# Another order of the first head pair's units, with two of its PSUM copies on ScalarE

## The chip, the core and the metric

The kernel runs on one core of a Trainium2 chip. The metric is the device time of one execution in microseconds (us); lower is better. TensorE multiplies matrices, VectorE and ScalarE read its results out of PSUM, GpSimd does small work, and DMA engines move and transpose data. A "slot" below is one place in the program's order, filled by one short unit of TensorE work.

## The reference, cut to what matters

```python
xn = layernorm(x)                                   # 2048 x 640
q  = xn @ wq                                        # 32 heads of 192
p  = softmax(q @ k[last 512].T * 192 ** -0.5)
s  = (p @ v[last 512]) @ wo                         # summed over the heads
g  = silu((silu(xn @ w_gate) * (xn @ w_up)) @ w_down)
return x + s * g
```

The kernel does the FFN g first, then attention in 16 pairs of heads, adding each pair's product with wo to s. The sums for s lie in SBUF as f32: s_m (columns 0 to 511, three of four row blocks), s_t (the last 128 columns, transposed) and s_o (the last block).

## The kernel before

After the FFN, each pair has two parts: scores and exponentials for four blocks of 512 rows, then a stretch of small units of TensorE work in a fixed order. A unit's name has the block, the kind and the half. Kinds a and b are the product of the probabilities with V, for row tiles 0-1 and 2-3. Kinds w, x and y are output products with wo of the block two before: row tiles 0-1, row tiles 2-3, and the last 128 columns. 0e is a query product of the next pair, moved forward. In the first pair only blocks 0 and 1 have output products, so they carry the names 2w, 2x, 2y and 3w, 3x, 3y.

The two halves of a unit use the two halves of TensorE's rows and swap PSUM banks between them. GpSimd's tiny memset passes the word from one half to the next, so another unit has to stand between the halves.

```python
def part(p):                                        # in pv(i, q2): kinds a and b
    ...
    st["acc"] = sc_tile() if i < 2 and q2 else mm_tile()   # two buffers in each pool
    ...
    if p == 3:
        divide(i, q2, acc, (0, 1) if i < 2 and q2 else ())

def divide(i, q2, acc, by_dve):                     # softmax's division, then a DMA transpose
    ...
    nc.vector.reciprocal(r[:], a_v[:, :, :, Dh : Dh + 1])
    ... # four ScalarE activations, or two VectorE multiplications, into O_b
    nc.sync.dma_start_transpose(out=OT_b[:, 6 * q2 : 6 * q2 + 6, :], in_=O_b[...])

def add_sum(pr, to, ps):
    if pr == 0:
        nc.vector.tensor_copy(out=to, in_=ps)       # first pair: a copy
    else:
        nc.vector.tensor_tensor(to, to, ps, ALU.add)

def sum_rows(i, qts, sc):                           # at the end of w and x
    ...
    add_sum(pr, to, sc)

FIRST = """0a0 0b0 0a1 0b1 0e0 1b0 1a0 1b1 2b0 1a1 2b1 2w0 2x0 2w1 2a0 2x1 2a1 2y0 3a0 3y0 3a1 3x0
    3b0 3x1 3w0 3b1 3w1"""                          # LATER is the order of the other pairs
```

The softmax here doesn't subtract the row's maximum and nothing guards it: scores larger than these inputs give would overflow.

## Time and profile before

| quantity | before |
|---|---|
| median time (3 runs, then 6 with those beside the changed kernel) | 923.19 us, then 923.16 us |
| span of the profiled run | 921.8 us |
| TensorE / VectorE / ScalarE busy | 914.7 / 594.6 / 473.7 us |
| the stretch of the first pair, first V product to next query product | 190.74 to 210.40 us |

The page's first part gives busy times, its fourth the chain of work that ended last. In a timeline, a line gives start, length, engine, line of the program and how many instructions are merged; the bracket gives the idle time ahead of it and what ended that. TensorE's ends are modelled: two units that follow each other without a pause start 0.65 to 0.67 us apart and are each shown as 0.81 to 0.83 us long. So a bracket on TensorE understates a loss by about 0.17 us. The length of the whole stretch does not have this fault.

Two more lines of the kernel before matter. The first is the group of VectorE's copies into s_m (line, engine, work, count, then busy us and mean ns of one, then idle time before them). The second tells how long the eight transposes of the stretch took from issue to landing.

```profile
L630 DVE COPY s_m<-sc 128x1024 f32<-128x1024 f32 x6 | 7.3, 1224 | 5.7 <-PE sc L619 5.6
DMA to landing us min/median/max: 2.7/2.8/4.6
```

The change takes two of those six copies. One of the eight transposes took 4.6 us where the median is 2.8.

### The profile page before, as it was taken

What the parts mean: (1) busy time and instruction counts of PE and PEld (TensorE: products, weight loads), DVE (VectorE), ACT (ScalarE), POOL (GpSimd) and SP (SyncE); (2) the same over time, 40 slices, a digit from 0 to 9 for tenths busy, and PEclk for the clock granted to TensorE, in tenths of its full rate; (3) what the DMA queues carried; (4) which work ended last, traced back from release to release, by engine and by line L of the source; (5) the groups of instructions that cost most, each with busy time, mean ns of one, the idle gap of its engine ahead of it and who ended that gap; (6) DMA issues with size and microseconds to landing.
All of it is one profiled execution on the core that took longest, in us unless ns stands there. A gap on an engine that the chain in (4) does not pass through costs nothing.

```text
span 921.8 us, 23762 instructions
## 1 busy us (share of the span) xinstructions
PE 914.7 (99%) x10193; PEld 527.3 (57%) x10193; DVE 594.6 (65%) x844; ACT 473.7 (51%) x841; POOL 91.0 (10%) x302
## 2 busy tenths in 40 slices
PE   9999999999999999999999999999999999999998
PEld 5444445564747464656565656565656565555664
DVE  6443321467676777777777767676767676767656
ACT  4222222546464656565655565655556565556561
POOL 0000000000000000000000000000000000002977
PEclk9999999999999999999999999999999999999999
DMA  9312430045443425343534453435353434333535
GB/s 310 68 34 65 90 78 1 1 67 121 51 112 47 111 56 104 58 103 58 108 58 108 57 109 57 97 58 97 69 95 65 92 75 76 89 70 108 127 48 163
DMA packets 246969, 77.45 MB, mean 84 GB/s; under 512 B 227792, under 2 KB 246864, under 8 KB 246864
## 3 DMA queue, kind: packets, MB, share of 16 engines
q1 hardware_dynamic: 245376, 74.23, 39.3%
q8 instruction: 80, 1.31, 0.6%
q10 hardware_dynamic: 1488, 1.70, 0.6%
q14 instruction: 25, 0.20, 0.1%
HBM read 39.06 MB, written 2.62 MB: 45 GB/s over the span
## 4 chain that ended last, share of the span: by engine, by line
PE 98%; DMA 1%; DVE 0%; SPq 0%; POOLq 0%; POOL 0%; issue 0%; DVEq 0%
PE mm L460 22%; PE sc L474 18%; PE sc L619 16%; PE mm L499 16%; PE sc L282 11%; PE mm L321 6%; PE sc L587 3%; PE sc L579 2%; PE mm L551 2%; PE mm L579 1%; DMA x_t<-in_A_x_dram 1%; DMA OT_b<-O_b 1%; PE gu L282 0%; PE mm L330 0%; PE sc L551 0%; PE sc L499 0%
## 5 line engine op out<-in xcount | busy, mean ns | idle before, releaser
L478 ACT ACTIVATE p_t<-sc 128x1024 bf16<-128x1024 f32 x254 | 253.3, 1024 | 120.2 <-PE sc L474 120.2
L465 DVE TENSOR_REDUCE qT<-mm 128x512 bf16<-128x1024 f32 x189 | 231.2, 1223 | 98.9 <-PE mm L460 96.4
L529 ACT ACTIVATE O_b<-mm,r 128x192 bf16<-128x192 f32 x490 | 166.5, 423 | 190.4 <-issue 138.9
L460 PE MATMUL mm<-xnT,wq_p 64*128 64x512 bf16 x1890 | 234.9, 376 | 0.0
L474 PE MATMUL sc<-qT,khat 64*128 64x512 bf16 x1524 | 195.4, 376 | 0.0
L619 PE MATMUL sc<-wo_p,OT_b 64*128 64x512 bf16 (+1 forms) x1608 | 179.2, 345 | 1.2 <-DMA OT_b<-O_b 1.2
L499 PE MATMUL mm<-V_p,p_t 64*128 64x193 bf16 x3520 | 178.3, 242 | 0.0
L499 PEld LDWEIGHTS <-p_t 64*128 64x128 bf16 x3584 | 155.0, 93 | 34.6
L460 PEld LDWEIGHTS <-wq_p 64*128 64x128 bf16 x1890 | 91.8, 94 | 112.0 <-issue 0.7
L632 DVE TENSOR_TENSOR s_m<-s_m,sc 128x1024 f32<-128x1024 f32 x82 | 100.2, 1222 | 49.3 <-PE sc L619 43.0
L474 PEld LDWEIGHTS <-khat 64*128 64x128 bf16 x1536 | 74.8, 94 | 91.0
L619 PEld LDWEIGHTS <-OT_b 64*128 64x128 bf16 x1608 | 75.6, 94 | 46.2 <-DMA OT_b<-O_b 1.7
L605 POOL MEMSET turn_t<- 128x1 f32 x246 | 24.4, 99 | 699.1 <-PE mm L499 494.2
L290 DVE TENSOR_TENSOR hT<-sc,sg 128x512 bf16<-128x512 f32 x46 | 31.7, 692 | 81.6 <-ACT sg L289 81.6
L632 DVE TENSOR_TENSOR s_t<-s_t,sc 128x512 f32<-128x512 f32 x82 | 56.2, 686 | 18.3 <-PE sc L587 16.8
L289 ACT ACTIVATE sg<-sc 128x512 bf16<-128x512 f32 x46 | 27.4, 597 | 69.7 <-PE sc L282 68.2
L282 PE MATMUL sc<-xnT,wg_sb 128*128 128x512 bf16 (+1 forms) x260 | 60.2, 354 | 0.1
L282 PE MATMUL sc<-xnT,wu_sb 128*128 128x512 bf16 (+1 forms) x260 | 60.2, 354 | 0.0
L632 DVE TENSOR_TENSOR s_o<-s_o,sc 128x640 f32<-128x640 f32 x52 | 42.7, 821 | 15.9 <-PE sc L619 14.8
L321 PE MATMUL mm<-wd_sb,hT 128*128 128x512 bf16 (+1 forms) x240 | 46.7, 347 | 0.0
L518 DVE RECIPROCAL r<-mm 128x4 f32<-128x4 f32 x124 | 22.6, 182 | 33.1 <-PE mm L499 24.7
L282 PEld LDWEIGHTS <-wu_sb 128*128 128x128 bf16 x285 | 27.0, 98 | 27.1 <-issue 0.3
(94 smaller groups left out, 458.9 us busy)
## 6 DMA issues: line engine op xcount, KB each, us to landing
wo_p<-in_A_wo_dram SPq DMA_DIRECT2D x16, 480.0 KB, 4.9
K_p<-in_A_k_cache_dram SPq DMA_DIRECT2D x32, 192.0 KB, 4.6
V_p<-in_A_v_cache_dram SPq DMA_DIRECT2D x32, 192.0 KB, 3.1
wq_p<-in_A_wq_dram SPq DMA_DIRECT2D x64, 80.0 KB, 2.9
wq_p<-in_A_wq_dram SPq DMA_DIRECT2D x16, 160.0 KB, 3.2
x_t<-in_A_x_dram SPq DMA_DIRECT2D x14, 160.0 KB, 3.1
OT_b<-O_b SPq DMA_TRANSPOSE x124, 2.7
wd_sb<-in_B_w_down_dram SPq DMA_DIRECT2D x1, 1920.0 KB, 11.8
```

Of the source, the lines that this page charges most:

```text
L282: nc.tensor.matmul(out, w_sb[:, c, f * P : (f + 1) * P], xnT[:, c, qc], start=(c == 0), stop=(c == NC - 1),)
L290: nc.vector.tensor_tensor(hTs[b][:, f, :], u, sg[:], ALU.mult)
L321: nc.tensor.matmul(dn, at, by, start=(f == 0), stop=(f == NF - 1))
L460: nc.tensor.matmul(q_ps[:, h, :], pairs[pr]["wq"][r, c, j * P : (j + 1) * P], xnT[r, c, b * 512 : (b + 1) * 512], start=(c == 0), stop=(c ...
L465: nc.vector.reduce_sum(qTs[i][:, j, :], q_ps[:, :, :].rearrange("p h n -> p n h"), axis=AX.X)
L474: nc.tensor.matmul(sc[:, h, :], khat[r, j, ks], qT[r, j, :], start=(j == 0), stop=(j == 2))
L478: nc.scalar.activation(p_t[:, :, :], sc[:, :, :], ACT.Exp, scale=scale)
L499: m = nc.tensor.matmul(acc[:, k, h * 256 : h * 256 + Dh + 1], Ps[i][kc][r, h, qt * P : (qt + 1) * P], V_p[r, kc, h, 0 : Dh + 1], start=(p ...
L529: nc.scalar.activation(O_b[:, qt, h, :], a_k[:, h, 0:Dh], ACT.Copy, scale=r[:, k, h, :])
L579: nc.tensor.matmul(ps, OTs[i][:, 3 * qt + j, :], pairs[i // NB]["wo"][:, j, cols], start=(first and j == 0), stop=(end and j == 2),)
L619: m = nc.tensor.matmul(ps[:, k, 0 : cols.stop - cols.start], OTs[i][r, 3 * qt + j, :], pairs[i // NB]["wo"][r, j, cols], start=(turn == 0 ...
L632: nc.vector.tensor_tensor(to, to, ps, ALU.add)
```

## The change

The order of the first pair's units is changed so that the first row tiles of block 2 come ahead of its second ones, while block 3 starts with its second row tiles. The copies of 2x and 3x go to ScalarE, which has more idle time in this stretch. The diff, whole:

```diff
@@ sum_rows
-        add_sum(pr, to, sc)
+        if i < 2 and qts.start:
+            nc.scalar.copy(to, sc)
+        else:
+            add_sum(pr, to, sc)
@@
-    FIRST = """0a0 0b0 0a1 0b1 0e0 1b0 1a0 1b1 2b0 1a1 2b1 2w0 2x0 2w1 2a0 2x1 2a1 2y0 3a0 3y0 3a1 3x0
-        3b0 3x1 3w0 3b1 3w1"""
+    FIRST = """0a0 0b0 0a1 0b1 0e0 1b0 1a0 1b1 2a0 1a1 2a1 2w0 2x0 2w1 2b0 2x1 3b0 2b1 3x0 2y0 3x1 3b1
+        3a0 3y0 3w0 3a1 3w1"""
```

## The prediction

> **What bounds the kernel now.** I read the page from the top: busy shares, the chain that ended last, then the chain and the timelines of the one stretch that the change touches. The first line below is the busy share of the engines, the second is the start of the chain's shares by line.
>
> ```profile
> PE 914.7 (99%) x10193; PEld 527.3 (57%) x10193; DVE 594.6 (65%) x844; ACT 473.7 (51%) x841; POOL 91.0 (10%) x302
> ...
> PE 98%; DMA 1%; DVE 0%; SPq 0%; POOLq 0%; POOL 0%; issue 0%; DVEq 0%
> ```
>
> TensorE is busy for 914.7 of the 921.8 us of the span, and 98% of the chain that ended last is TensorE. VectorE, at 65%, and ScalarE, at 51%, do not bound it. A change that leaves TensorE's work as it is can win at most the 7.1 us in which TensorE idles, and most of that is the start and the end of the program. The change touches the value and output products of the first head pair only. This stretch runs once, between about 190.7 us (the first product with V_p) and 210.4 us (the next product with wq_p). The chain of waits there:
>
> ```profile
> 193.57 1.08 PE mm L460 x10
> 194.65 0.67 PE sc L499 x16
> 195.32 0.57 PE mm L499 x13
> 195.89 4.62 DMA OT_b<-O_b
> 200.51 0.05 issue
> 200.55 1.47 PE sc L619 x12
> ```
>
> One link is not TensorE's: the transpose of a block's divided outputs, issued at 195.89 us and landed 4.62 us later. The timeline of TensorE (start, length, work, and in brackets the idle time before it) shows what it costs and that nothing else is lost:
>
> ```profile
> 198.49 0.81 PE L619 MATMUL sc<-wo_p,OT_b 64*128 64x512 bf16 x6
> 200.55 1.47 PE L619 MATMUL sc<-wo_p,OT_b 64*128 64x512 bf16 x12 [1.25 <-DMA OT_b<-O_b]
> 201.86 0.83 PE L499 MATMUL mm<-V_p,p_t 64*128 64x193 bf16 x16
> 202.53 0.81 PE L619 MATMUL sc<-wo_p,OT_b 64*128 64x512 bf16 x6
> 203.17 0.83 PE L499 MATMUL mm<-V_p,p_t 64*128 64x193 bf16 x16
> ...
> 209.75 0.81 PE L619 MATMUL sc<-wo_p,OT_b 64*128 64x512 bf16 x6
> 210.40 1.24 PE L460 MATMUL mm<-xnT,wq_p 64*128 64x512 bf16 x10
> ```
>
> The idle time is 1.25 us, ahead of what the code calls 2x0, the first half of the output product of block 0's second two row tiles. Starts of neighbouring units are 0.65 us apart where the first is six output matmuls and 0.67 us where it is sixteen value matmuls. From 200.55 to 210.40 us lie nine of the one and six of the other: 9 x 0.648 + 6 x 0.667 = 9.83 us, against 9.85 us measured. So after the DMA wait there is no idle time left to remove. VectorE's and ScalarE's timelines of the same stretch:
>
> ```profile
> 202.06 2.54 DVE L630 COPY s_m<-sc 128x1024 f32<-128x1024 f32 x2 [3.18 <-PE sc L619]
> ...
> 208.64 1.22 DVE L630 COPY s_m<-sc 128x1024 f32<-128x1024 f32 x1 [1.10 <-PE sc L619]
> ...
> 210.60 1.22 DVE L630 COPY s_m<-sc 128x1024 f32<-128x1024 f32 x1 [0.47 <-PE sc L619]
> 211.74 1.21 DVE L465 TENSOR_REDUCE qT<-mm 128x512 bf16<-128x1024 f32 x1
> 204.73 1.36 ACT L529 ACTIVATE O_b<-mm,r 128x192 bf16<-128x192 f32 x4 [2.76 <-DVE r L518]
> ```
>
> The four VectorE copies are those that the change's condition picks from; ScalarE idles for 2.76 us in between, so it has room for two of them.
>
> **What the Trainium skill says.** "Perfetto Trace Analysis" (Identifying the Most-Contended Engine) says to optimize the engine with the most occupancy first, and that matmul busy time overstates how near the limit TensorE is. Here busy time is used only to find gaps, for which back-to-back starts suffice. "ScalarE: Activation LUTs" (What ACT_TABLE_LOAD costs) gives 0.833 ns per element and a fixed 186 ns when scale and bias are immediates, and its section Table sets: the hidden batching unit has copy in every set, so no table load is added. The trace of before agrees roughly: the exponentials of 128x1024 take 1025 ns at the median, casts of 128x512 from PSUM take 587 ns. "PSUM — Partial Sum Buffer" (Specifications (TRN2)) says ScalarE and VectorE can read PSUM in parallel if their banks do not collide; ScalarE's divisions and VectorE's copies overlap in this trace at unchanged lengths (the second copy of the pair at 202.06 us is 1.22 us as well). "Runtime: NRT & Kernel Launch" (Instruction fetch mechanics) says engines fetch instructions in blocks of 16 KiB, 256 instructions, through DMA. The packet records agree: the queue marked instruction moved 80 packets of 16 KB, and one of them, at 197.88 us, took 0.92 us in the middle of the late transpose. Eighteen of that transpose's 256-byte packets took 1.7 to 1.9 us, while the mean of packets in an undisturbed transpose is about 20 ns.
>
> **The change part by part.** A unit is written as block, kind, half: a and b are the value products of row tiles 0-1 and 2-3; w and x are output products of row tiles 0-1 and 2-3, y that of the last 128 columns, all three of the block two before the one in their name.
>
> Removed: two VectorE copies of 128x1024, 2 x 1.22 = 2.45 us of VectorE, those of 2x and 3x. Added: two ScalarE copies. From the cast and the exponential (1025 - 587) / 512 = 0.86 ns per element, so an estimate of 1.02 us each, 2.04 us of ScalarE. TensorE's instructions are the same in number and kind. Moved: 2a now runs where 2b ran and 2b where 2a ran or one place later; 3b and 3x come forward, 3a and 3y go back. Up to 2x1 each place holds a unit of the same length as before.
>
> The wait of 1.25 us: its transpose, the transposes ahead of it and the lengths of all units ahead of it are unchanged. The instruction orders compared, with their waits, give TensorE's first difference at row 2645, 68 rows after 2x0's first. The instruction fetch that delays the transpose follows TensorE's position in its own program, so it should fall at the same place. Gain: 0.
>
> After it, I lay the new order out from 200.55 us with the same unit times: 2x0 200.55, 2w1 201.21, 2b0 201.86, 2x1 202.53, 3b0 203.17, 2b1 203.84, 3x0 204.51, 2y0 205.16, 3x1 205.80, 3b1 206.45, 3a0 207.12, 3y0 207.78, 3w0 208.43, 3a1 209.08, 3w1 209.75, next pair 210.40. Each unit that opens a PSUM tile needs the tile two openings earlier in its pool read out. A unit's results are ready 0.81 us (outputs) or 0.83 us (values) after its start, and the reader starts 0.02 us later:
> - 2b0 (201.86) needs 1a divided: done 199.61, unchanged. 3b0 (203.17) needs 2a divided: ScalarE's four divisions start at 200.61, when the transpose lands, end 201.97. Slack 1.2 us.
> - 3x0 (204.51) needs 2w copied by VectorE: 202.06 + 1.22 = 203.29. Slack 1.2 us.
> - 2y0 (205.16) needs 2x copied by ScalarE: 202.53 + 0.83 + 1.02 = 204.38. Slack 0.8 us.
> - 3a0 (207.12) needs 2b divided: values ready 204.67, reciprocal to 204.87, four divisions of 1.36 us to 206.26. Slack 0.9 us.
> - 3y0 (207.78) needs 3x copied by ScalarE: 3x1 starts 205.80, the copy 206.63, and it ends 207.65. Slack 0.1 us. This is the tightest, and the only one tighter than before, where the shortest slack was that of 3x0 on 2y's copy and addition (206.47 - 206.13 = 0.3 us).
> - 3w0 (208.43) needs 2y copied and added: 205.99 + 0.69 + 0.69 plus 0.04 = 207.41. Slack 1.0 us.
> - The next pair's first product (210.40) needs 3b divided, 209.02, and the second (212.77) 3a divided, 211.6. Its second score tile (212.12) needs 3w copied by VectorE, 211.82, as now.
>
> Every one holds, so the stretch ends at 210.40 us again, and 3w's copy is still what VectorE does ahead of the next reduction at 211.74 us. Nothing after it has changed order. The 2.45 us taken from VectorE lie beside TensorE, as do the 2.04 us on ScalarE. Sum on the path: 0 us, with up to 0.15 us of wait ahead of 3y0 if the ScalarE copy takes 1.2 us like VectorE's. 923.19 + 0.0 = 923.2 us.
>
> **The rivals.**
> (1) A new wait takes the place of none: ScalarE's copy of 3x is late for 3y0. For it: the slack of 0.1 us is an estimate on a copy that no line of this trace has (f32 to f32). Against it: the exponential of the same shape is 1025 ns. It would make 923.3 to 923.5 us.
> (2) The 1.25 us wait goes or grows. The collision of the fetch with the transpose is a matter of tenths of a microsecond: the transpose's packets start at 197.08 and its undisturbed run is about 1.1 us, so a fetch 0.4 us later would miss it. Its usual time to landing is 2.8 us, which gives 198.7 instead of 200.51 us, before 2x0 could start at 199.14. That would make 923.19 - 1.25 = 921.9 us. For it: the runs of before lie 0.9 us apart (923.14 and 924.0), so something moves by that much. Against it: nothing ahead of that point changes, so both kernels should share it.
> (3) VectorE was holding PSUM tiles in this stretch and its relief shortens it by several tenths. For it: two copies back to back, 2.54 us. Against it: no idle time on TensorE between 200.55 and 210.40 us. It would make 922.9 us if it were so.
>
> **Range and chances.** The step that could matter is bounded by one stretch of 20 us in 923. The whole of it idle-free is worth -1.25 us, a new wait +0.15 us, and the spread of the runs of before is 0.9 us, upward. I put the range at 922.3 to 924.1 us. To leave the 2% band the time would have to move by 18.5 us, about the length of the stretch itself, and only the changed build's going wrong in a way that no view shows would do that: faster 0.01, same 0.98, slower 0.01.
>
> **What would show it right or wrong.** Right: TensorE's timeline has the bracket of about 1.25 us ahead of the output matmuls near 200.5 us, no further bracket to 210.4 us, and the next product with wq_p starts at 210.4 us; two ScalarE copies of 128x1024 of about 1.02 us at 203.4 and 206.6 us, and four VectorE copies to s_m instead of six in the whole run. VectorE's busy time falls by 2.4 us, ScalarE's rises by 2.0, TensorE's stays at 914.7. Wrong: a bracket naming ScalarE ahead of L587 near 207.8 us (rival 1), the DMA bracket gone or larger (rival 2), or the stretch shorter with that bracket unchanged (rival 3). A difference over 1.5 us in the median would mean that something outside this stretch moved, which I hold to be excluded.

## The result

| | before | changed |
|---|---|---|
| median of 6 runs | 923.16 us (922.87 to 924.0) | 923.07 us (922.79 to 923.37) |
| ratio | | 0.9999, 95% interval 0.9986 to 1.0011 |
| span of the profiled run | 921.8 us | 921.6 us |
| VectorE / ScalarE busy | 594.6 / 473.7 us | 592.4 / 475.1 us |
| length of the stretch | 19.66 us | 19.53 us |

A ratio here is the mean time of one kernel's fast runs over that of the other's of the same rounds, so it is not quite the ratio of the medians.

The kernel takes the same time. Its chain of waits in the stretch still goes through the same transpose:

```profile
195.22 0.56 PE mm L499 x13
195.78 4.50 DMA OT_b<-O_b
200.28 0.05 issue
200.32 1.47 PE sc L619 x12
```

TensorE's timeline of the changed kernel:

```profile
198.40 0.81 PE L619 MATMUL sc<-wo_p,OT_b 64*128 64x512 bf16 x6
200.32 1.47 PE L619 MATMUL sc<-wo_p,OT_b 64*128 64x512 bf16 x12 [1.12 <-DMA OT_b<-O_b]
201.63 0.83 PE L499 MATMUL mm<-V_p,p_t 64*128 64x193 bf16 x16
...
207.56 0.81 PE L587 MATMUL sc<-OT_b,wo_p 64*128 64x512 bf16 x6
208.21 0.81 PE L619 MATMUL sc<-wo_p,OT_b 64*128 64x512 bf16 x6
...
210.17 1.24 PE L460 MATMUL mm<-xnT,wq_p 64*128 64x512 bf16 x10
```

The first two lines are 2w0 and 2x0 with the wait between them, as before; the bracket is 1.12 us instead of 1.25. From 2x0 to the next query product it is 9.85 us, as before, so no new wait came. The lines at 207.56 and 208.21 are 3y0 and 3w0, where the prediction saw the tightest slack: they follow without a pause. ScalarE's timeline of the same stretch, and below it VectorE's:

```profile
203.15 1.01 ACT L641 COPY s_m<-sc 128x1024 f32<-128x1024 f32 x1 [1.41 <-PE sc L619]
...
206.43 1.01 ACT L641 COPY s_m<-sc 128x1024 f32<-128x1024 f32 x1 [0.37 <-PE sc L619]
```

```profile
206.52 0.69 DVE L632 TENSOR_TENSOR s_t<-s_t,sc 128x512 f32<-128x512 f32 x1
...
210.37 1.23 DVE L630 COPY s_m<-sc 128x1024 f32<-128x1024 f32 x1 [0.44 <-PE sc L619]
```

The two copies run on ScalarE for 1.01 us each and fit into its idle time. 3w's copy is still VectorE's last work of the stretch. VectorE's group of copies into s_m, which had six before, has four:

```profile
L630 DVE COPY s_m<-sc 128x1024 f32<-128x1024 f32 x4 | 4.9, 1225 | 4.4 <-PE sc L619 4.4
```

So the change moved work off an engine that held nothing up. What is left of interest is the one wait of the stretch: what it comes from, whether the order or the copies could touch it, and how close the new order runs to another wait.

### The profile page after: what moved, and what is told of

Same layout as the page of the kernel before. It is cut to its first block, busy times and chain, and to the rows that moved or that the text cites. A ratio compares the mean times of both kernels' runs of the same rounds, so it can differ in the third digit from the quotient of the medians.

```text
span 921.6 us, 23742 instructions
## 1 busy us (share of the span) xinstructions
PE 913.3 (99%) x10172; PEld 527.0 (57%) x10193; DVE 592.4 (64%) x842; ACT 475.1 (52%) x843; POOL 90.7 (10%) x302
## 4 chain that ended last, share of the span: by engine, by line
PE 98%; DMA 1%; DVE 0%; issue 0%; SPq 0%; POOLq 0%; POOL 0%; DVEq 0%
PE mm L460 22%; PE sc L474 18%; PE sc L619 16%; PE mm L499 16%; PE sc L282 11%; PE mm L321 6%; PE sc L587 3%; PE mm L551 2%; PE sc L579 2%; PE mm L579 1%; DMA x_t<-in_A_x_dram 1%; DMA OT_b<-O_b 0%; PE gu L282 0%; PE mm L330 0%; PE sc L551 0%; PE sc L499 0%
```

## The experiments

**What the packet records show.** In both traces a 16 KB packet of the queue marked instruction (a "fetch" below) is in flight together with the late transpose. Of the kernel before, 219 transposes have a known landing. In 55 of them a fetch, of 16 KB or of the second instruction queue's 8 KB, overlaps the time from 1.0 to 2.3 us after their issue, and their median to landing is 3.84 us; the other 164 have 2.72 us. In the changed kernel it is 3.83 us (49) against 2.72 us (170). This is a correlation. Five of the other 164 are late too (3.4 to 4.5 us). Two of these do meet a fetch, which begins 2.3 and 2.4 us after their issue, and two were issued 1.4 and 1.8 us behind a late one. The fifth (issued at 906.2 us, 4.1 us to landing) meets none, so fetches are not the only cause of lateness in the whole run.

The packets also show how the two are tied. In ten transposes (the second one of the stretch in the eight traces with 0 or 256 rows more, the third one with 160 rows, the first one with 40; these runs are told below) 18 to 22 of the 256-byte packets are held. They come free 0.8 to 0.9 us after the fetch has ended, and the transpose lands 1.68 to 1.76 us after that end, although the fetch begins anywhere from 1.1 to 2.0 us after the issue. So the landing follows the end of the fetch. That fits the tenth of a microsecond between the two kernels' waits: the fetch ended 2.91 us after the issue before, 2.75 in the changed kernel.

The experiments tell three theories apart: the wait is the fetch's, and neither order nor copies touch it; or the wait has another cause; or VectorE's relief is worth something. Every kernel gave a correct result.

All runs, with times read from their traces. "Fetch" is when the 16 KB fetch nearest to the second transpose of the stretch (the one 2x0 waits for) began. "Landing" is that transpose's time from issue to landing. "Stretch" is the length defined above.

| run | fetch, us | landing, us | bracket ahead of 2x0, us | stretch, us | median time beside the kernel before, us |
|---|---|---|---|---|---|
| before | 197.88 | 4.62 | 1.25 | 19.66 | 923.16 |
| changed | 196.93 | 4.50 | 1.12 | 19.53 | 923.07 beside 923.16 |
| order alone | 196.76 | 4.61 | 1.22 | 19.82 | 923.63 beside 923.20 |
| ScalarE copies alone | 196.67 | 4.54 | 1.16 | 19.57 | 923.19 beside 923.20 |
| changed, 160 rows more | 199.28 | 2.74 | none | 18.23 | 922.35 beside 923.20 |
| changed, 256 rows more | 197.00 | 4.43 | 1.05 | 19.46 | 924.07 beside 923.20 |
| changed, 80 rows more | 194.54 | 2.75 | none | 18.23 | 922.24 beside 923.36 |
| changed, 40 rows more | 195.15 | 3.82 | see below | 18.84 | 923.40 beside 923.16 |
| before, 80 rows more | 194.57 | 2.76 | none | 18.23 | 922.31 beside 923.16 |
| changed, 3y earlier | 196.70 | 4.73 | 1.36 | 20.16 | 923.68 beside 923.36 |
| order without waits | 196.31 | 4.54 | no unit waits there | 18.33 | 921.56 beside 923.36 |
| changed, again | 196.57 | 4.56 | 1.18 | 19.58 | 922.94 beside 923.36 |

**Order alone (e1_order_only).** All copies stay on VectorE.

```diff
-        if i < 2 and qts.start:
-            nc.scalar.copy(to, sc)
-        else:
-            add_sum(pr, to, sc)
+        add_sum(pr, to, sc)
```

> The new order with all copies left on VectorE. Theory (the order is free only because ScalarE takes the copies): VectorE works in program order, so the copy of 3x stands behind 2y's copy and addition, which end about 207.3 us, and ends about 208.5; 3y, which needs that PSUM tile and could start at 207.6, waits 0.9 us. A bracket of 0.8 to 1.0 us naming VectorE ahead of the L587 product near 208.4 us, the DMA bracket of 1.1 to 1.3 us unchanged, time 0.9 us over the kernel before, about 924.0. Rival (VectorE never held the stretch and order does not matter): no second bracket, 923.1 us.

Measured: 923.63 us, ratio 1.0004 with interval 0.999 to 1.0019. This missed. TensorE's timeline of the run (first fence) shows no bracket after the DMA wait, and 3y0 starts while VectorE still copies 3x (second fence, VectorE's timeline):

```profile
207.44 0.81 PE L587 MATMUL sc<-OT_b,wo_p 64*128 64x512 bf16 x6
208.28 0.82 PE L619 MATMUL sc<-wo_p,OT_b 64*128 64x512 bf16 x6
```

```profile
207.01 1.22 DVE L630 COPY s_m<-sc 128x1024 f32<-128x1024 f32 x1
```

So 3y0 does not take 3x's tile. The next unit, 3w0, does: it starts 0.84 us after 3y0 instead of 0.65, just after the copy ends at 208.23. Of the expected 0.9 us, 0.19 are real. The ScalarE copies of the change save that much in the new order; the timed runs are too coarse to show it.

**ScalarE copies alone (e2_scalar_only).** The FIRST of before, the rest as changed.

```diff
-    FIRST = """... 1b1 2a0 1a1 2a1 2w0 2x0 2w1 2b0 2x1 3b0 2b1 3x0 2y0 3x1 3b1 ..."""
+    FIRST = """... 1b1 2b0 1a1 2b1 2w0 2x0 2w1 2a0 2x1 2a1 2y0 3a0 3y0 3a1 3x0 ..."""
```

> The old order with the two copies on ScalarE. Theory (VectorE's copies lie beside TensorE): nothing to gain, one DMA bracket of 1.1 to 1.3 us, no other, time within 0.3 us of the kernel before, 923.1. Rival (VectorE's relief is worth something by itself): 0.2 us or more faster, 922.9 or less, with the stretch from the first output product to the next wq_p product shorter than 12 us less the bracket.

Measured: 923.19 us beside 923.20, ratio 1.0001, interval 0.9986 to 1.0016, one DMA bracket of 1.16 us and no other. VectorE's relief by itself shows no worth here; the stretch is 0.09 us shorter than that of the kernel before, as is the DMA bracket. That rival falls.

```profile
200.06 1.47 PE L619 MATMUL sc<-wo_p,OT_b 64*128 64x512 bf16 x12 [1.16 <-DMA OT_b<-O_b]
```

**The fetch moved (e3_fetch_moved) and brought back (e4_fetch_back).** If the fetch follows TensorE's position in its own program, in blocks of 256 rows, then rows added anywhere ahead of the stretch move it. It did: it began 6.3 us after the start of the stretch in the changed kernel, 5.0 us with 40 rows more, 3.7 with 80, 2.2 with 160 and 6.3 again with 256, where the page also counts 81 such packets instead of 80. I halved the columns of FFN products, which adds weight loads and matmuls but no columns. No wait is taken away.

```diff
             for s in range(2):
-                hidden_mm(gu[s], s, f, slice(b * 512, (b + 1) * 512))
+                n = 2 if b == 1 and f < 8 else 1
+                for k in range(n):
+                    at = slice(k * 512 // n, (k + 1) * 512 // n)
+                    hidden_mm(gu[s][:, at], s, f, slice(b * 512 + at.start, b * 512 + at.stop))
```

The second run also halves four down products (96 rows), which makes 256 rows in all, one whole block.

> The changed kernel with 80 more TensorE matmuls and weight loads 130 us before the stretch, made by halving the columns of eight units of the FFN, same columns in all: 160 more instruction rows, so the blocks of 256 rows end elsewhere. Theory (a 16 KB instruction fetch in flight at the same time slows the transpose): the fetch falls about 3 us earlier, near 194, and about 200 to 201; the transpose issued near 195.8 lands in 2.7 to 3.0 us; the bracket ahead of 2x0 is 0 to 0.2 us; the stretch is 1.1 us shorter, and the time 0.5 to 1.1 us lower where the halving costs nothing. Rival (the transpose is late because of the other transposes issued behind it, or of PSUM traffic): the bracket stays at 1.1 to 1.3 us.

> The same as the run with the fetch moved, plus 96 more rows from four halved down products: 256 rows more than the changed kernel, one whole block. Theory (fetch): the fetch is back at its place relative to the stretch, so the transpose is late again, 4.3 to 4.7 us to landing, and the bracket is 1.0 to 1.3 us. Rival (the halving itself, not the place of the fetch, removed the bracket): the bracket stays away as in the run before it.

Measured with 160 rows more: the transpose lands in 2.74 us, and 2w0, 2x0 and 2w1 run as one group of 18 matmuls without a bracket in TensorE's timeline.

```profile
198.62 2.11 PE L622 MATMUL sc<-wo_p,OT_b 64*128 64x512 bf16 x18
...
209.09 1.24 PE L463 MATMUL mm<-xnT,wq_p 64*128 64x512 bf16 x10
```

(Lines are three higher because of the edit.) The fetch that began at 193.08 was over before the second transpose was issued. The next one, at 199.28, now meets the next transpose, which took 4.5 us to land, and nobody waits for that one. The time is 922.35 us, ratio 0.9991, interval 0.9977 to 1.0006: the size expected, though the interval includes 1. With 256 rows more, the bracket is back in TensorE's timeline:

```profile
200.35 1.47 PE L628 MATMUL sc<-wo_p,OT_b 64*128 64x512 bf16 x12 [1.05 <-DMA OT_b<-O_b]
```

So it is the place of the fetch that counts and not the halving. Two of its four timed runs are slower than expected (924.68 and 924.70 us, where the profiled one took 923.46); what delays them I did not find, as the profiled run does not show it.

**The fetch elsewhere (e8_fetch_on_first, e10_fetch_between).** Four and two FFN units halved, that is `f < 4` and `f < 2` in the diff above.

> The changed kernel with four FFN units halved, 80 more rows: the fetch moves to about 195.3 us, onto the first transpose (issued 194.4) instead of the second. Theory (fetch): the first transpose lands in 3.8 us or more, near 198.5 instead of 197.2, the second at most at 199.9, and the brackets ahead of 2w0 and 2x0 together are 0.3 to 1.2 us. Rival (only the second transpose can be late, for a reason of its own, and the halving of eight units happened to remove it): the first lands in 2.8 us, the second in 4.5 us, bracket 1.1 us ahead of 2x0 alone.

> The changed kernel with two FFN units halved, 40 more rows. The fetch began at 196.9 with 0 more rows and at 194.5 with 80, so near 195.7 here, while the first transpose's packets move (195.7 to 196.8 us). Theory (a fetch in flight slows whichever transpose it meets): the first transpose, issued near 194.5, lands after 3.6 us or more instead of 2.8; the bracket ahead of 2w0 or 2x0 is up to 1.2 us. Rival (only the second transpose of the stretch can be late): the first lands in 2.8 us and the second in 4.3 us or more.

With 80 rows the fetch came at 194.54 us and was over at 195.50, before the first transpose's packets start (issued at 194.63; in the kernel before they start 1.2 us after the issue). Neither transpose was late and the bracket was gone:

```profile
198.57 2.10 PE L622 MATMUL sc<-wo_p,OT_b 64*128 64x512 bf16 x18
```

I had aimed at the first transpose and missed it by a microsecond, so this run tells only that a fetch ahead of both is harmless. With 40 rows it came at 195.15 and lasted 1.33 us. Then the first transpose (issued 193.93, landed 198.23) took 4.31 us, twenty of its packets taking 1.3 to 1.6 us, and the second, behind it, 3.82 us. In TensorE's timeline the bracket moves to 2w0:

```profile
198.28 2.31 PE L622 MATMUL sc<-wo_p,OT_b 64*128 64x512 bf16 x18 [0.24 <-DMA OT_b<-O_b]
...
893.64 1.47 PE L582 MATMUL sc<-wo_p,OT_b 128*128 128x512 bf16 x6 [1.05 <-DMA OT_b<-O_b]
```

The group of 18 lasts 2.31 us instead of 2.11, a second wait of 0.2 us inside it. The stretch is 0.7 us shorter than in the changed kernel. The second line shows where time was lost again: at the end of the same run another fetch (891.57 us) is in flight while another transpose is waited for, a wait that the changed kernel's trace does not have. From the end of the stretch to the end of the program this trace has 712.6 us, every other one 711.4 to 711.5. Moving fetches in one place moves them in all.

**The kernel before with the fetch moved (e11_before_fetch_moved).** The edit of 80 rows on the kernel before.

> The kernel before, order and copies as they were, with four FFN units halved, 80 more rows. Theory (the DMA wait is the fetch's and has nothing to do with order or copies): no bracket on TensorE in the stretch, second transpose landed in 2.7 to 3.0 us, time 922.1, about 1.1 us less than the kernel before. Rival (the kernel before needs the new order or the ScalarE copies to profit): a bracket of 0.3 us or more naming VectorE or DMA, 922.7 or more.

Measured: 922.31 us beside 923.16, ratio 0.9989, interval 0.9976 to 1.0003, no bracket in TensorE's timeline:

```profile
198.65 2.10 PE L622 MATMUL sc<-wo_p,OT_b 64*128 64x512 bf16 x18
...
209.13 1.24 PE L463 MATMUL mm<-xnT,wq_p 64*128 64x512 bf16 x10
```

With the old order and the old copies the stretch is 18.23 us, to the hundredth the same as with the new ones. Without the late transpose both orders are free of waits, so neither the order nor the copies had anything to win.

**3y earlier (e5_3y_earlier).** After the miss of the first run, this one tells which tile 3y takes.

```diff
-        3a0 3y0 3w0 3a1 3w1"""
+        3y0 3a0 3w0 3a1 3w1"""
```

> The changed kernel with 3y moved ahead of 3a, one place of 0.67 us. It tells which tile 3y takes. Theory now (a pool hands out the tile that was released first in program order, so 3y takes 2y's, released by VectorE's addition, which ended at 207.21 us in the changed kernel): 3y can start at 207.25 where its place is at 206.9, a bracket of 0.3 to 0.4 us naming VectorE, relative to the same start of the stretch. Rival (the recorded prediction: 3y takes 3x's tile, released by ScalarE's copy, which ended at 207.44): a bracket of 0.5 to 0.6 us naming ScalarE.

TensorE's, VectorE's and ScalarE's timelines of this run, one line of each:

```profile
207.13 0.83 PE L587 MATMUL sc<-OT_b,wo_p 64*128 64x512 bf16 x6 [0.21 <-DVE s_t L632]
```

```profile
206.39 0.69 DVE L632 TENSOR_TENSOR s_t<-s_t,sc 128x512 f32<-128x512 f32 x1
```

```profile
206.29 1.01 ACT L641 COPY s_m<-sc 128x1024 f32<-128x1024 f32 x1 [0.37 <-PE sc L619]
```

3y0 waits for VectorE and starts at 207.13, right after 2y's addition ends at 207.08, while ScalarE's copy of 3x still runs until 207.30. The unit before it started at 206.08 and two value halves take 0.67 us, so its place was 206.75 and it lost 0.38 us, of which the bracket shows 0.21. The tile is 2y's. The changed kernel's trace says the same: 3y0's first weight load waits on a semaphore that VectorE raises, 3w0's first matmul on one that ScalarE raises.

**An order without waits (e6_no_wait_order), and the changed kernel again (e9_changed_again).** With the rule for tiles put right, I wrote down the measured lengths of the units, divisions, copies and transposes and searched by program for an order in which nothing waits even when the transpose is late. All four s_m copies of the stretch are on ScalarE.

```diff
-        if i < 2 and qts.start:
+        if i < 2:
@@
-    FIRST = """0a0 0b0 0a1 0b1 0e0 1b0 1a0 1b1 2a0 1a1 2a1 2w0 2x0 2w1 2b0 2x1 3b0 2b1 3x0 2y0 3x1 3b1
-        3a0 3y0 3w0 3a1 3w1"""
+    FIRST = """0a0 0b0 0a1 1a0 0b1 1a1 1b0 0e0 1b1 2a0 2w0 2b0 2w1 2a1 2y0 2x0 2b1 2x1 3x0 3b0 3a0 3x1
+        3w0 3b1 3y0 3w1 3a1"""
```

> An order laid out so that the transpose of block 0's second half has work ahead of it until 0.8 us after its late landing, with all four 128x1024 copies on ScalarE. Theory (the DMA wait is the only loss of the stretch, and work placed ahead of it hides it whatever the fetch does): no bracket over 0.1 us on TensorE in the stretch, the next pair's first wq_p product 1.1 us earlier than in the changed kernel relative to the first product with V_p (18.4 instead of 19.5 us), time 922.0, ratio 0.9988. Rival (the late transpose or another wait moves with it): a bracket of 0.3 us or more elsewhere, 922.6 or more.

> The changed kernel unaltered, to time it five rounds on the same chip as the order without waits. Theory: same as before within 0.3 us, 923.1, with the DMA bracket of 1.0 to 1.3 us. Rival (some gain hidden in the scatter of the first six runs): 922.8 or less with an interval that excludes 1.

TensorE's timeline of the order without waits:

```profile
190.02 0.83 PE L499 MATMUL mm<-V_p,p_t 64*128 64x193 bf16 x16
...
199.07 0.83 PE L499 MATMUL mm<-V_p,p_t 64*128 64x193 bf16 x16
199.84 0.83 PE L587 MATMUL sc<-OT_b,wo_p 64*128 64x512 bf16 x6
...
208.35 1.26 PE L460 MATMUL mm<-xnT,wq_p 64*128 64x512 bf16 x10
```

The second transpose is as late as ever (4.54 us), but the first unit to need it, 2y0, is due only when it lands (199.705) and loses 0.10 us: 0.77 us after its forerunner instead of 0.67. The stretch takes 18.33 us instead of 19.53. The time is 921.56 us beside 923.36, ratio 0.9984, interval 0.997 to 0.9998. It is the fastest kernel and the only one whose interval excludes 1, though 0.2% is far from the 2% that counts as faster. Not all of it is the order's: of the 2.0 us between the profiled spans (919.8 and 921.8) the stretch gives 1.32, and 0.72 lie ahead of it, where the two programs are the same. The start of the stretch scatters from 190.0 to 190.9 us over the traces here, and is 190.64 and 190.19 in two traces of the changed kernel. So the order is worth about 1.3 us. The changed kernel, timed in the same rounds, is at ratio 0.9999 again (0.9987 to 1.0012).

## Why the prediction was right

The prediction was right: 923.2 us foreseen, 923.07 measured, "same" foreseen and found. Step by step:

- **No idle time after the DMA wait.** Confirmed: 2x0 to the next query product takes 9.85 us in both kernels, and the kernel before with the fetch moved has no wait at all in the stretch.
- **The 1.25 us stay.** Confirmed at 1.12, and by the second look at the changed kernel at 1.18. The reason given, that the fetch meets the transpose at the same place, holds in kind. Its time was off: the fetch began 0.95 us earlier (196.93 instead of 197.88 us) though TensorE's rows ahead of it are the same. The place is thus not as fixed as the prediction took it to be, though in all eight traces with 0 or 256 rows more the fetch began 1.1 to 2.0 us after the second transpose's issue and made it late. That the fetch causes the lateness was an inference from one packet; the runs with 160, 256, 80 and 40 more rows and the one on the kernel before show it.
- **ScalarE's copies at an estimated 1.02 us, in its idle time.** Measured 1.01 us each. No table load came with them: both traces have three, the last at 168 us. The line given for "unchanged lengths" does not show it: no division runs beside the second copy of the pair at 202.06 us. The copy at 208.64 us (1.22 us, while divisions run from 207.62 to 208.98) does.
- **VectorE less 2.45 us, ScalarE more by 2.04.** Measured 2.2 less and 1.4 more. The copies themselves are as foreseen (two fewer of 1.22 us, two more of 1.01); the rest is scatter of other groups between two profiles, such as 0.3 us in the exponentials.
- **TensorE's busy time stays at 914.7.** The page shows 913.3, but with 10172 matmul records instead of 10193 and the same 10193 weight loads. Twenty-one records are missing from the trace, so this sign can't be judged.
- **The table of slacks.** Here a step was wrong, without weight for the result. It said that a unit "needs the tile two openings earlier in its pool read out". The pool hands out the tile that was released first in the program's order. 3x opens before 2y but is released after it. So 3y takes 2y's tile and 3w takes 3x's, which the runs of the order alone and of 3y earlier show. The entry "3y0 needs 3x copied by ScalarE, slack 0.1 us" should read: 3y0 needs 2y added by VectorE, which ended at 206.52 + 0.69 = 207.21, against a start at 207.56, a slack of about 0.35 us. 3w0 (208.21) needs 3x copied, 207.44, about 0.8 us. Rival 1 was built on the wrong entry, and so was the 0.9 us expected of the order alone.
- **Rival 2**, the wait going away with the fetch, was the one with substance: 921.9 us foreseen if the wait went, 922.2 to 922.4 us measured in the three runs in which the fetch was moved clear of it. Its margin was too small: "0.4 us later" would be 2.4 us after the issue, and in the trace of the kernel before three of the eight 16 KB fetches that begin 2.3 to 2.5 us after an issue still go with a landing of 4.2 to 4.5 us (one of these also met an 8 KB fetch).
- **Rival 3**, VectorE holding tiles, fell with the run of ScalarE copies alone.

## What to carry to other kernels

When TensorE has no idle time in a stretch, look for what each of its waits hangs on before moving work between other engines: here a new order and 2.2 us less work on VectorE gained nothing, while one late transpose held 1.4 us. A wait that hangs on a chance meeting of two transfers can be hidden by putting independent work ahead of it: the order without waits lost 0.10 us though the transpose was as late as ever (it was not tried with the fetch elsewhere). Moving the meeting (by adding instructions) helps one place and can hurt another. For slack tables, follow the order in which buffers are released in the program, not that in which they are opened.

## What the Trainium skill lacked or had wrong

- "Runtime: NRT & Kernel Launch", Instruction fetch mechanics: it says that crossing a 16 KiB boundary costs one bump of a DMA tail, "mostly hidden". No run here shows TensorE waiting for its instructions, but the fetch occupies DMA for 0.9 to 1.7 us and a transpose that it meets takes 3.84 us at the median instead of 2.72 (219 transposes of the kernel before). Here that made brackets of 1.1 to 1.4 us on TensorE. It also gives 16 KiB for the block; 25 packets of the second instruction queue are of 8 KB.
- "DMA: Bandwidth & Descriptors", DMA Transpose (X-bar): it has no word on a transpose meeting an instruction fetch. The runs show 18 to 22 of its 256-byte packets held for 1.3 to 2.0 us at once, against about 20 ns for the mean packet of an undisturbed one.
- No page says how closely a fetch keeps to its place in the instruction order. "Runtime: NRT & Kernel Launch", Instruction fetch mechanics, only says that markers stand at block boundaries; with the same TensorE rows ahead of it, it began between 6.3 and 7.1 us after the start of the stretch in the kernels with 0 or 256 more rows.
